# Bonus and decayed keys of two chunks formed on TensorE, and corner products in every chunk

## The chip, the cores and the metric

The kernel runs on one core of one Trainium2 chip. The metric is the device time of one execution in microseconds. A profile of one execution gives the busy times and waits of the engines: TensorE (PE, with its weight loads as PEld), VectorE (DVE), ScalarE (ACT), GpSimd (POOL) and SyncE (SP, which issues nearly all transfers here).

## What is computed

The reference is an attention layer with a decaying state, followed by a feed-forward network (FFN) with a maximum over three products. There are 4 batches, 8 heads, 768 tokens and 48 features a head; the FFN goes from 384 to 768 and back.

```python
for t in range(S):
    kt, vt, rt = (k[:, :, t], v[:, :, t], r[:, :, t])
    cur = np.einsum('bhd,bhe->bhde', u[None] * kt, vt)
    y[:, :, t] = np.einsum('bhd,bhde->bhe', rt, state + cur)
    state = w[None, :, :, None] * state + np.einsum('bhd,bhe->bhde', kt, vt)
...
h = np.maximum(np.maximum(x @ w1, x @ w2), x @ w3)
return (h @ w_out).astype(np.float32)
```

## The kernel before, in words

The 768 tokens are cut into 12 chunks of 64 tokens. Within a chunk the recurrence is written as products of matrices. Keys and receptances are scaled by powers of w (`kT`, `rT`, "by feature": features on partitions, tokens along the row). Their product is the **scores**, of which the strict triangle is kept; on the diagonal stands the **bonus**, the sum over features of r u k for one token. The **values** are the masked scores times v, plus the receptances times the state of the chunk before. The **keys** step multiplies keys that are decayed to the chunk's end (by token: tokens on partitions) with v and adds the product to the decayed state.

A chunk's work is done in two halves q, each of two head pairs and four batches, so eight units; one unit's two heads lie on partitions 0 to 63 and 64 to 127.

- Chunks 0 and 1 (`c < WHOLE`) are computed in float32 by `whole` (L514): for each unit two matmuls, on the upper left and the lower right corner of the array.
- From chunk 2 on, each operand is split into a high and a low half-precision part, and `split` forms three products of them. For `c < CORNERS`, 2 to 5, it does this on the two corners too (L507). For chunks 6 to 11 it does one matmul on the whole array (L504), with the stationary operand laid out as two blocks on a diagonal (`kb`, `ktb`, `vb`, `sb`); SyncE spreads it there from `kd`, `ktd`, `vd`, `sd` by two transfers each (`spread`, L403).
- The bonus of every chunk is formed by token: `product` (L468, L469: r times u, times k), `total` (L473: the sum over features) and `diagonal` (L482, or on ScalarE in chunks 1 and 2 L480), which writes a tile `am` with the sum on the diagonal. `mask` (L529) then copies the strict triangle of the scores into it.
- The decayed keys are formed by token: `decay` (L488) multiplies k with a table `tkt`. This table is made at the start from powers of w: `tkf`, four transposes on TensorE (`turn`, L381), and a scaled copy back on ScalarE (`turned_back`, L387).
- For each half `load_feat` fetches k and r by feature, and `load_tok` k, r and v by token.
- `into_state` takes the keys into the state (for chunk 0 a copy on ScalarE, L555). The tile `state` is cleared once by GpSimd (L422), as the last of the clearings that begin the program.
- `x_high` and `x_low` (L579, L583) leave the values as two half-precision parts in x; `x_last` (L590) moves the last rows by six small transfers.
- The FFN of a chunk is 162 matmuls up and 54 down, each 128x256 (L606), 216 together. The eight weight blocks arrive as float64 words and are turned into high and low half-precision parts by `tops`, `convert`, `round_up` and `leave` (L332, L336, L339, L342); three buffers hold the raw words.
- `stir` (L602) issues matmuls on zeros that fill TensorE early in the program.

The order of the work on every engine is laid down by a planner written in the kernel, `Plan`. Each step has a due time, an engine and a cost; the step that can begin first is taken, and among those that can begin together the one with the least due time. A table `SHIFT` moves the due times of a kind of step in five stages of the program. Attention of chunk c + 1 is planned among the FFN matmuls of chunk c. In the program each engine then takes its own steps in that order, and waits for what the next step in it needs.

Of the kernel before, what the change touches and what calls it, by code (L numbers as in the profile page):

```python
# [7 lines left out]
F32 = mybir.dt.float32  # L8
# [10 lines left out]
P = 128  # L19
# [9 lines left out]
CORNERS = 6  # L29
# [42 lines left out]
class Plan:  # L72
# [7 lines left out]
        "sp feat": (-1.49, 2.17, 0.19, -3.89, 0),  # L80
        "sp tok": (-1.09, 1.99, -1.51, 4.86, 0),
        "pe blank": (-0.88, 0, 0, 0, 0),
        "pe turned": (-0.6, 0, 0, 0, 0),
        "act tkt": (-3.41, 0, 0, 0, 0),
        "dve kT": (-1119.88, -1756.78, 0, 0, 0),
        "dve rT": (-1334.71, -15, 3.25, 0, 0),
        "dve am": (-1125.06, 1.34, 2.16, 2.05, -2.59),
        "dve a": (-2132.64, 1.4, 16.62, -0.32, 3.81),
        "pe sc": (0.03, -10.26, 30.66, -0.53, 1.03),
        "pe va": (0.91, 1.78, -0.08, 0.01, 0.84),  # L90
        "act xh": (-8.58, -4.39, 1.75, 1.33, -5.9),
        "dve xl": (16.85, -38.36, -0.44, -3.2, 5.06),
        "sp x3": (0.32, -1.77, -0.27, 5.34, 0),
        "act xsq": (0, 6.53, -0.6, 3.25, 26.15),
        "pe stir": (0, 0.37, 2.53, -0.41, -0.95),
        "sp word": (-0.57, -0.37, 0, 0, 0),
        "act ztop": (-7.39, -7.43, 0, 0, 0),
        "dve word": (-7.71, -14.92, 0, 0, 0),
        "act his": (58.47, -2.11, 0, 0, 0),
        "dve lo": (-35.68, -11.65, 0, 0, 0),  # L100
        "dve kdec": (-2131.57, 30.7, -5.18, 0, 0),
        "pe ke": (16.12, -0.08, -1.91, 0.38, 0),
        "act state": (0, -9.9, 0, 0, 0),
        "act sq": (0, -89.13, 2.23, 16.37, 24.01),
        "dve sd": (0, 2.02, 0, 0, 0),
        "act am": (0, 4.85, 3.9, 0, 0),
        "dve state": (0.52, 9.7, 0.2, -1, 0),
        "act sdh": (-0.93, -1.27, -0.92, 3.4, 0),
        "dve sdl": (-2.26, -11.65, -8.71, 1.59, 0),
        "pe up": (0, -2.28, 0, 0.17, 16.73),  # L110
        "act m": (0.86, 0.59, 4.26, -3.44, 1.05),
        "dve m": (5.69, -20.85, 12.62, -4.02, -0.89),
        "act hh": (0.73, -0.55, -2.83, -2.22, 1.5),
        "pool hl": (-0.73, -0.35, -5.98, -1.87, 1.73),
        "dve hl": (0, 1.96, -1.92, -1.11, -5.26),
        "pe dn": (0, -9.28, -5.13, 0.33, 0.9),
        "act io": (0, 1.12, -0.87, 1.27, 0.35),
        "sp io": (0, 0.08, -3.87, -0.2, 0.45),
        "act kdh": (0, 0.19, 6.03, 1.49, 1.44),
        "dve kdl": (0, -5.27, -1.57, 0.94, 3.23),  # L120
        "act rh": (0, 2.85, 1.75, 8.52, -0.79),
        "dve rl": (0, 3.84, -1.29, 6.17, -0.44),
        "act ah": (0, -1.76, 6.26, 15.54, 3.78),
        "dve al": (0, 0.87, 2.5, -0.18, 2.31),
        "act ktdh": (0, -6.24, 14.69, -1.38, 0),
        "dve ktdl": (0, 10.62, -0.11, -0.11, 0),
        "act vdh": (0, 5.83, 4.84, 9.54, 0.19),
        "dve vdl": (0, 0.77, 6.47, 1.1, -3.32),
        "pool kT": (0, 0, -0.51, -11.37, 0),
        "pool rT": (0, 0, -5.5, -2.61, 0.38),  # L130
        "pool am": (0, 0, -6.41, -29.97, -0.42),
        "pool kdec": (0, 0, 3.41, 2.45, 0),
        "sp sb": (0, 0, 0, -3.01, 0),
        "sp kb": (0, 0, 0, -8.27, 4.47),
        "sp ktb": (0, 0, 0, 0.67, 0),
        "sp vb": (0, 0, 0, 0.11, -1.09),
        "act wsq": (0, 0, 0, 7.12, 0),
        "sp again": (0, 0, 0, 0, 3.09),
        "dve ends": (0, 0, 0, 0, 2.23),
        "dve good": (0, 0, 0, 0, -0.78),  # L140
        "pe count": (0, 0, 0, 0, -2.69),
        "dve flag": (0, 0, 0, 0, -3.04),
# [99 lines left out]
def kernel(ctx, tc, feat, tok, wu, ut, ws, wo, cst, out):  # L242
# [34 lines left out]

    wu_sb = const.tile([P, 2, NP], F32, name="wu_sb")
# [105 lines left out]
    def turned_back():  # L384
        for hh in range(2):
            hs = slice(hh * C, (hh + 1) * C)
            nc.scalar.mul(out=tkt[hs], in_=turned[0][hs, :, hh * C:hh * C + D], mul=SC_KT)  # L387
# [138 lines left out]

    def mask(c, q):
        t = raws[c, q]
        nc.vector.copy_predicated(out=t["a"], mask=strict.unsqueeze(1).broadcast_to([P, U, C]), data=t.pop("sc"))  # L529
# [254 lines left out]
    plan = Plan(dict(feat=2, tok=3, raw64=3, psa=2, psv=2, psm=4, rh=2, rl=2, am=2, a=2, ah=1, al=1, x=2, m=3, io=3, hh=1, hl=1))  # L784
# [99 lines left out]
    def whole_scores(c, q, due):  # L884
# [19 lines left out]
    def keyed(c, q, due, reads):  # L904
        do(due, "pe", 1.35 if c < WHOLE else 0.79 if c < CORNERS else 0.62, lambda: keys(c, q), reads=reads, takes=[("psv", ("ke", c, q))], counts=0.5 if c < WHOLE else 1.0)
# [13 lines left out]
    def valued(c, q, due, reads):  # L919
        reads = [*reads, *held(c, [("sdh", q), ("sdl", q)], ("sb", q))]  # L920
        do(due, "pe", 1.58 if c < CORNERS else 1.42, lambda: values(c, q), reads=[*reads, ("ah", c, q), ("al", c, q), ("rh", c, q), ("rl", c, q)], takes=[("psv", ("va", c, q))])
# [77 lines left out]
    for q in range(2):  # L999
        fetched(0, q, -3 + 0.1 * q)  # L1000
        do(-4, "pe", 1.0, blank, takes=[("psv", ("blank", q))])
    do(-0.55, "pe", 0.55, turn, takes=[("psa", "turned")])
    do(-0.54, "act", 0.7, turned_back, reads=["turned"], writes=["tkt"])
# [92 lines left out]
```

## Time and profile before

| What | Value |
|---|---|
| Median of 3 runs | 395.57 us (395.3 to 395.86) |
| Profiled execution, time | 395.38 us |
| Profiled execution, span | 393.6 us |
| PE busy | 373.2 us, 95% |
| DVE busy | 257.0 us, 65% |
| ACT busy | 240.0 us, 61% |
| POOL busy | 189.2 us, 48% |
| Mean granted TensorE clock | 0.983 |
| Moved by DMA | 70.56 MB |

The span goes from the first to the last instruction that the profile holds; the time of the execution has a little more around it. "Idle before" in a row is the time in which the engine waited in front of an instruction, and the name behind the arrow is what ended the wait. PE's ends are modelled, so starts of neighbouring rows are the better ruler.

### The profile page before, as it was taken

The page shows a single profiled execution, that of the slowest core. Times are in us where ns is not written, and L with a number is a line of the kernel's source. Part 1 is how long each engine was busy: PE and PEld are TensorE (multiplying, and loading weights), DVE is VectorE, ACT ScalarE, POOL GpSimd, SP SyncE. Part 2 cuts the span into 40 slices and gives each one's busy share as a digit, 9 for nine tenths or more (in the row PEclk, how much of TensorE's full clock was granted, in tenths as well). Part 3 has the DMA queues.
Part 4 walks back from the last instruction along what each step waited for, and adds up shares of the span by engine and source line. Part 5 has one row for each costly group of instructions (what it writes and reads, how often), then busy time and mean ns, then how long its engine had stood idle before and what let it go on. Part 6 is the DMA issues. An engine that isn't in the chain of part 4 may idle for free.

```text
span 393.6 us, 13760 instructions
## 1 busy us (share of the span) xinstructions
PE 373.2 (95%) x5780; PEld 332.4 (84%) x5780; DVE 257.0 (65%) x475; ACT 240.0 (61%) x622; POOL 189.2 (48%) x187
## 2 busy tenths in 40 slices
PE   4977799899999999999999999999999999999994
PEld 3866688788888888888999999999999999988883
DVE  7699889888857567676776757658559545232350
ACT  2376876696656556556666556646564954697621
POOL 9600112499897646656566656656748311011110
PEclk9996899999999999999999999999999999999998
DMA  8976380730623423484993996995997874822201
GB/s 293 418 257 244 127 339 15 254 130 10 199 81 113 153 70 99 146 207 124 272 276 108 254 295 166 255 278 160 279 294 194 231 183 90 271 78 84 75 2 48
DMA packets 25430, 70.56 MB, mean 179 GB/s; under 512 B 4368, under 2 KB 11536, under 8 KB 24336
## 3 DMA queue, kind: packets, MB, share of 16 engines
q1 hardware_dynamic: 25216, 69.51, 59.2%
q8 instruction: 47, 0.77, 0.8%
q14 instruction: 23, 0.19, 0.2%
q10 hardware_dynamic: 144, 0.10, 0.1%
HBM read 39.95 MB, written 4.72 MB: 113 GB/s over the span
## 4 chain that ended last, share of the span: by engine, by line
PE 80%; DVE 8%; ACT 5%; POOL 4%; issue 1%; ACTq 0%; POOLq 0%
PE psm L606 66%; PE psv L504 6%; PE psv L507 4%; DVE w L342 2%; PE psa L504 2%; ACT ztop L332 2%; PE psa L507 2%; DVE raw L336 2%; ACT w L339 1%; DVE feat L449 1%; ACT junk L432 1%; POOL ztop L323 1%; ACT am L480 1%; POOL ktd L398 0%; POOL vd L398 0%
## 5 line engine op out<-in xcount | busy, mean ns | idle before, releaser
L606 PEld LDWEIGHTS <-w 128*128 128x128 f16 x2592 | 250.3, 98 | 32.8 <-issue 2.7
L606 PE MATMUL psm<-x,w 128*128 128x256 f16 x1944 | 224.0, 274 | 2.2 <-ACT m L621 2.1
L634 POOL TENSOR_TENSOR hl<-m,hh 128x256 f16<-128x256 f32 x60 | 49.8, 830 | 149.1 <-ACT hh L628 145.4
L625 DVE SCALAR_TENSOR_TENSOR m<-psm,m 128x256 f32<-128x256 f32 x144 | 60.4, 421 | 58.5 <-PE psm L606 48.6
L628 ACT CAST hh<-m 128x256 f16<-128x256 f32 x72 | 29.0, 402 | 57.3 <-DVE m L625 56.6
L449 POOL TENSOR_TENSOR feat<-feat,wrt 128x512 f32<-128x512 f32 x36 | 51.2, 1434 | 12.2 <-DMA feat<-in_feat_dram 12.0
L606 PE MATMUL psm<-hh,w 128*128 128x256 f16 x432 | 56.3, 273 | 0.0
L432 ACT ACTIVATE junk<-tok 128x384 bf16<-128x384 f32 x72 | 37.3, 518 | 2.2 <-DMA tok<-in_tok_dram 1.4
L621 ACT ACTIVATE m<-psm 128x256 f32<-128x256 f32 x72 | 27.2, 379 | 11.8 <-PE psm L606 10.7
L606 PE MATMUL psm<-hl,w 128*128 128x256 f16 x216 | 33.4, 273 | 0.0
L468 POOL TENSOR_TENSOR am<-tok,u_sb 128x384 f32<-128x384 f32 x18 | 18.4, 1020 | 20.1 <-DVE al L539 20.1
L583 DVE SCALAR_TENSOR_TENSOR x<-psv,x 112x512 f16<-112x512 f32 x24 | 16.4, 685 | 12.7 <-ACT x L579 12.6
L473 DVE TENSOR_REDUCE a<-am 128x8 f32<-128x384 f32 x24 | 13.2, 550 | 17.6 <-POOL am L469 17.5
L651 ACT ACTIVATE io<-psm 128x256 f32<-128x256 f32 x36 | 13.4, 382 | 16.8 <-PE psm L606 16.5
L482 POOL TENSOR_TENSOR am<-cs,a 128x512 f32<-128x512 f32 x18 | 19.7, 1092 | 7.6 <-DVE a L473 7.3
L529 DVE COPY_PREDICATED am<-cs,psa 128x512 f32<-128x512 int32 x24 | 17.5, 731 | 8.8 <-PE psa L504 7.2
L579 ACT ACTIVATE x<-psv 112x512 f16<-112x512 f32 x24 | 14.2, 590 | 12.4 <-PE psv L504 6.4
L417 DVE TENSOR_TENSOR kd<-feat,kd 128x512 f16<-128x512 f32 x20 | 18.9, 946 | 3.5 <-ACT kd L412 3.4
L469 POOL TENSOR_TENSOR am<-am,tok 128x384 f32<-128x384 f32 x18 | 18.9, 1047 | 1.4
L488 POOL TENSOR_TENSOR tok<-tok,tkt 128x384 f32<-128x384 f32 x16 | 18.6, 1162 | 0.5 <-ACT junk L432 0.5
L417 DVE TENSOR_TENSOR ktd<-tok,ktd 128x384 f16<-128x384 f32 x18 | 15.3, 850 | 4.9 <-DMA sb<-sd 2.3
L412 ACT ACTIVATE kd<-feat 128x512 f16<-128x512 f32 x20 | 12.5, 627 | 8.8 <-POOL feat L449 8.8
(110 smaller groups left out, 604.9 us busy)
## 6 DMA issues: line engine op xcount, KB each, us to landing
tok<-in_tok_dram SPq DMA_DIRECT2D x30, 576.0 KB, 5.9
feat<-in_feat_dram SPq DMA_DIRECT2D x24, 512.0 KB, 4.3
raw<-in_ws_dram SPq DMA_DIRECT2D x6, 1152.0 KB, 7.8
out_dram<-io SPq DMA_DIRECT2D x36, 128.0 KB, 4.6
kb<-kd SPq DMA_DIRECT2D x12, 256.0 KB, 6.4
sb<-sd SPq DMA_DIRECT2D x12, 256.0 KB, 6.7
vb<-vd SPq DMA_DIRECT2D x12, 256.0 KB, 7.5
kb<-kd SPq DMA_DIRECT2D x12, 248.0 KB, 6.6
```

What stands on the lines that cost most here:

```text
L417: nc.vector.tensor_tensor(out=dense.dense[:, 1, :, 0:w], in0=src, in1=dense.dense[:, 0, :, 0:w], op=ALU.subtract)
L432: nc.scalar.activation(out=junk[:, 0:U * D].rearrange("p (u d) -> p u d", u=U), in_=src, func=AF.Square, scale=scale, accum_out=stat[:, ki ...
L449: helper(c).tensor_tensor(out=t[n], in0=t[n], in1=tb, op=ALU.mult)
L469: helper(c).tensor_tensor(out=w, in0=w, in1=units(t["k"]), op=ALU.mult)
L482: helper(c).tensor_tensor(out=t["a"], in0=eye.unsqueeze(1).broadcast_to([P, U, C]), in1=t.pop("sum").unsqueeze(2).broadcast_to([P, U, C]), ...
L504: nc.tensor.matmul(out=ps[:, i, :], lhsT=block[k].on[a][i], rhs=prods[k](b, i), **flags)
L507: nc.tensor.matmul(out=ps[h][0:n, i, :], lhsT=dense[k].dense[h, a, i, 0:n], rhs=prods[k](b, i)[h], **flags)
L606: nc.tensor.matmul(out=ps, lhsT=a, rhs=b, start=first and n == 0, stop=last and n == len(prods) - 1)
L621: nc.scalar.mul(out=m, in_=ps, mul=by)
L625: nc.vector.scalar_tensor_tensor(out=m, in0=ps, scalar=by, in1=m, op0=ALU.mult, op1=ALU.max)
L628: nc.scalar.copy(out=h[0][:, f, :], in_=m)
L634: lows_by(c, f).tensor_tensor(out=h[1][:, f, :], in0=m, in1=h[0][:, f, :], op=ALU.subtract)
```

## The change

For chunks 0 and 1 neither k nor r is loaded by token; only v is (`load_v`). The bonus is formed by TensorE from the operands by feature: `r_u` multiplies the scaled receptances with u w (on ScalarE), `bonus` multiplies the scaled keys with that (32 float32 matmuls for each half), and `on_diagonal` keeps the diagonal of the result (on VectorE). The decayed keys by token are formed by `flipped`, a float32 product of the scaled keys with a diagonal matrix `dg`, and copied and scaled by ScalarE (`flipped_back`). `product`, `total`, `diagonal` and `decay` remain for chunks 2 to 11, and `tkf`, `turn` and `turned_back` become steps of the plan with later due times.

`CORNERS` goes from 6 to 12, so that `split` uses corners in every chunk from 2 on and no operand is spread any more. The clearing of the blocks kb, ktb, vb and sb by GpSimd stays. Costs of several steps in the plan and the whole table `SHIFT` are new.

```diff
-CORNERS = 6
+CORNERS = 12
...
     SHIFT = {
-        "sp feat": (-1.49, 2.17, 0.19, -3.89, 0),
...
+        "sp feat": (1.97, 1.58, -2.27, 4.37, 0),
...
+    def load_v(c, q):
+        t = raw.tile([P, 2, B, D], F32, name="v1", bufs=4)
+        nc.sync.dma_start(out=t, in_=tok[c, q][:, 2])
+        raws.setdefault((c, q), {}).update(v=t)
...
-    tkf = hp.tile([P, NP, 2, C], F32, name="hl")
-    for hh in range(2):
-        nc.vector.tensor_tensor(out=tkf[:, :, hh, :], in0=pw[:, :, 0:C][:, :, ::-1], in1=pw[:, :, C // 2].unsqueeze(2).broadcast_to([P, NP, C]), op=ALU.mult)
+    uw = const.tile([P, NP], F32, name="uw")
+    nc.vector.tensor_tensor(out=uw, in0=uf_sb, in1=w_sb, op=ALU.mult)
+    dg = const.tile([P, NP, D], F32, name="dg")
+    nc.vector.tensor_tensor(out=dg, in0=eye[:, 0:D].unsqueeze(1).broadcast_to([P, NP, D]), in1=wc.unsqueeze(2).broadcast_to([P, NP, D]), op=ALU.mult)
+    tkf = const.tile([P, NP, 2, C], F32, name="tkf")
+
+    def both():
+        for hh in range(2):
+            nc.vector.tensor_tensor(out=tkf[:, :, hh, :], in0=wkt, in1=wck.unsqueeze(2).broadcast_to([P, NP, C]), op=ALU.mult)
...
+    def r_u(c, q):
+        t = raws[c, q]
+        t["ru"] = work.tile([P, U, C], F32, name="ru")
+        for g in range(2):
+            nc.scalar.mul(out=t["ru"][:, g * B:(g + 1) * B, :], in_=t["rT"][:, g], mul=uw[:, 2 * q + g:2 * q + g + 1])
+
+    def bonus(c, q):
+        t = raws[c, q]
+        t["bo"] = psa.tile([P, U, C], F32, name="psa")
+        whole(t["bo"], C, (units(t["kT"]), t.pop("ru")))
+
+    def on_diagonal(c, q):
+        t = raws[c, q]
+        t["a"] = work.tile([P, U, C], F32, name="am", bufs=2)
+        nc.vector.tensor_tensor(out=t["a"], in0=t.pop("bo"), in1=eye.unsqueeze(1).broadcast_to([P, U, C]), op=ALU.mult)
+
+    def flipped(c, q):
+        t = raws[c, q]
+        t["kp"] = psa.tile([P, U, D], F32, name="psa")
+        for i in range(U):
+            for h in HS:
+                nc.tensor.matmul(out=t["kp"][h, i, :], lhsT=units(t["kT"])[h, i, :], rhs=dg[h, 2 * q + i // B, :], start=True, stop=True)
+
+    def flipped_back(c, q):
+        t = raws[c, q]
+        t["kt"] = work.tile([P, U, D], F32, name="kt")
+        nc.scalar.mul(out=t["kt"], in_=t.pop("kp"), mul=SC_KT / SC_R)
...
-            whole(t["ke"], D, (units(t["k"]), units(t["v"])))
+            whole(t["ke"], D, (t.pop("kt"), units(t["v"])))
...
+        if c < WHOLE:
+            dma(due, lambda: load_v(c, q), 0.85, reads=behind, writes=["fetched"], takes=[("v1", ("tok", c, q))])
+            return
...
+        if c < WHOLE:
+            do(due - 0.30, "pe", 0.76, lambda: flipped(c, q), reads=[("feat", c, q), ("kT", c, q)], takes=[("psa", ("kp", c, q))], counts=0.5)
+            do(due - 0.30, "act", act(U * D), lambda: flipped_back(c, q), reads=[("kp", c, q)], takes=[("kt", ("kt", c, q))])
+            return [t, ("kt", c, q)]
...
-        before_mask(c, q, due)
+        do(due - 0.27, "act", 2 * act(U * C // 2), lambda: r_u(c, q), reads=[f, ("rT", c, q)], takes=[("ru", ("ru", c, q))])
+        do(due - 0.27, "pe", 0.96, lambda: bonus(c, q), reads=[f, ("kT", c, q), ("ru", c, q)], takes=[("psa", ("bo", c, q))], counts=0.5)
+        do(due - 0.26, "dve", 0.64, lambda: on_diagonal(c, q), reads=[("bo", c, q)], takes=[("am", ("am", c, q))])
...
-    do(-0.55, "pe", 0.55, turn, takes=[("psa", "turned")])
-    do(-0.54, "act", 0.7, turned_back, reads=["turned"], writes=["tkt"])
+    do(0.1, "dve", 0.7, both, writes=["tkf"])
+    do(0.12, "pe", 0.55, turn, reads=["tkf"], takes=[("psa", "turned")])
+    do(0.14, "act", 0.7, turned_back, reads=["turned"], writes=["tkt"])
```

More of the change, by code (lines that the diff above doesn't have):

```diff
@@ L79 @@
     SHIFT = {
-        "sp feat": (-1.49, 2.17, 0.19, -3.89, 0),
[L81 to L121, printed above, removed]
@@ L133 @@
[L133 to L142, printed above, removed]
+        "sp feat": (1.97, 1.58, -2.27, 4.37, 0),
+        "sp tok": (-3.45, -1.24, -1.61, 3.67, 0),
@@ new lines @@
+        "pe blank": (-2.18, 0, 0, 0, 0),
+        "dve tkf": (0, 1.52, 0, 0, 0),
+        "pe turned": (0, 0.11, 0, 0, 0),
+        "act tkt": (0, -0.35, 0, 0, 0),
+        "dve kT": (-0.86, -9.38, 0, 0, 0),
+        "dve rT": (7.54, 0.51, 8.81, 0, 0),
+        "act ru": (-0.05, -0.44, 0, 0, 0),
+        "pe bo": (-4.05, 1.51, 0, 0, 0),
+        "dve am": (0, 5.93, 5.68, -3.51, 0),
+        "pe sc": (-2.13, -0.6, -4.99, -0.28, -2.15),
+        "pe va": (0.51, -10.53, -1.39, 0.02, -0.01),
+        "act xh": (0, 1.96, -5.35, -1.01, -2.13),
@@ L143 @@
+        "act wsq": (0, 0, 0, -0.02, -0.56),
+        "sp again": (0, 0, 0, 0, 3.74),
+        "dve ends": (0, 0, 0, 0, 2.93),
+        "dve good": (0, 0, 0, 0, -11.99),
+        "pe count": (0, 0, 0, 0, 0.31),
+        "dve flag": (0, 0, 0, 0, -4.22),
     }
@@ L386, in turned_back @@
             hs = slice(hh * C, (hh + 1) * C)
-            nc.scalar.mul(out=tkt[hs], in_=turned[0][hs, :, hh * C:hh * C + D], mul=SC_KT)
+            nc.scalar.copy(out=tkt[hs], in_=turned[0][hs, :, hh * C:hh * C + D])
     class Block:
@@ L781, in general @@
                     put(m, leaving(ps, P, 1.0))
-    plan = Plan(dict(feat=2, tok=3, raw64=3, psa=2, psv=2, psm=4, rh=2, rl=2, am=2, a=2, ah=1, al=1, x=2, m=3, io=3, hh=1, hl=1))
+    plan = Plan(dict(feat=2, tok=3, raw64=3, v1=4, ru=1, kt=1, psa=2, psv=2, psm=4, rh=2, rl=2, am=2, a=2, ah=1, al=1, x=2, m=3, io=3, hh=1, hl=1))
     do = plan.do
@@ L892, in whole_values @@
         sbs = [("sd", q), ("rT", c, q), ("feat", c, q)] if c else []
-        do(due, "pe", 1.35 * (1 + (c > 0)), lambda: values(c, q), reads=[("am", c, q), ("tok", c, q), *sbs], takes=[("psv", ("va", c, q))], counts=0.5)
+        do(due, "pe", 0.92 * (1 + (c > 0)), lambda: values(c, q), reads=[("am", c, q), ("tok", c, q), *sbs], takes=[("psv", ("va", c, q))], counts=0.5)
         leave_x(c, q, due)
     def scored(c, q, due, reads):
-        do(due, "pe", *((1.75,) if c < WHOLE else (0.79,) if c < CORNERS else (0.72,)), lambda: scores(c, q), reads=reads, takes=[("psa", ("sc", c, q))], counts=0.5 if c < WHOLE else 1.0)
+        do(due, "pe", 0.96 if c < WHOLE else 0.8 if c < CORNERS else 0.72, lambda: scores(c, q), reads=reads, takes=[("psa", ("sc", c, q))], counts=0.5 if c < WHOLE else 1.0)
         do(due + 0.02, "dve", dve(U * C), lambda: mask(c, q), reads=[("sc", c, q)], writes=[("am", c, q)])
@@ L904, in keyed @@
     def keyed(c, q, due, reads):
-        do(due, "pe", 1.35 if c < WHOLE else 0.79 if c < CORNERS else 0.62, lambda: keys(c, q), reads=reads, takes=[("psv", ("ke", c, q))], counts=0.5 if c < WHOLE else 1.0)
+        do(due, "pe", 0.76 if c < WHOLE else 0.64 if c < CORNERS else 0.62, lambda: keys(c, q), reads=reads, takes=[("psv", ("ke", c, q))], counts=0.5 if c < WHOLE else 1.0)
         s = ("state", q)
@@ L920, in valued @@
         reads = [*reads, *held(c, [("sdh", q), ("sdl", q)], ("sb", q))]
-        do(due, "pe", 1.58 if c < CORNERS else 1.42, lambda: values(c, q), reads=[*reads, ("ah", c, q), ("al", c, q), ("rh", c, q), ("rl", c, q)], takes=[("psv", ("va", c, q))])
+        do(due, "pe", 1.43 if c < CORNERS else 1.42, lambda: values(c, q), reads=[*reads, ("ah", c, q), ("al", c, q), ("rh", c, q), ("rl", c, q)], takes=[("psv", ("va", c, q))])
         leave_x(c, q, due)
```

61 lines of the change are left out of this document (47 added, 14 removed).

## The prediction

> **What bounds the kernel now.** I read the page's totals, then the span cut into stages, then TensorE and ScalarE in order of time where the stages lose time, and last the chain in the steady part. The profiled execution took 395.38 us for a span of 393.6 us, so 1.8 us lie around the span, and its time is 0.2 us under the median of 395.57 us. The sum below is made against 395.38. A difference under 0.2%, 0.8 us, can't be told from none.
>
> First the page's total of TensorE and the stages (columns: stretch, length, busy time of PE, weight load, DVE, ACT and POOL with their instructions, granted clock, DMA share, GB/s).
>
> ```profile
> PE 373.2 (95%) x5780; PEld 332.4 (84%) x5780; DVE 257.0 (65%) x475; ACT 240.0 (61%) x622; POOL 189.2 (48%) x187
> 0.00:16.00 16.00, 10.54 (x113) 7.93 (x114) 11.63 (x29) 2.29 (x4) 15.45 (x21) 1.00 0.90 345
> 16.00:35.68 19.68, 14.47 (x277) 12.73 (x274) 17.13 (x25) 13.37 (x27) 0.00 (x0) 0.83 0.80 285
> 35.68:48.20 12.52, 10.40 (x153) 8.55 (x150) 10.41 (x13) 11.79 (x21) 0.01 (x1) 0.86 0.35 132
> 48.20:71.20 23.00, 22.37 (x288) 19.26 (x285) 21.02 (x38) 16.94 (x38) 4.78 (x5) 1.00 0.45 169
> 71.20:80.00 8.80, 7.68 (x238) 6.88 (x236) 6.56 (x15) 5.85 (x18) 5.35 (x5) 1.00 0.86 301
> 80.00:387.80 307.80, 307.73 (x4728) 277.00 (x4725) 190.28 (x361) 189.40 (x517) 163.64 (x157) 1.00 0.60 166
> ```
>
> From 80 us to 387.8 us TensorE is busy 307.73 of 307.80 us at full clock: no other engine and no transfer is waited for there, so this part gets longer by whatever is added to TensorE and can't be shortened by relief elsewhere. Before it lies the start: up to 35.68 us TensorE has no FFN work at all, and from there to 80 us it loses 44.3 - 10.4 - 22.4 - 7.7 = 3.9 us idle and some more at a clock of 0.86 up to 48 us. The change works on both parts: it takes work off the start, and turns chunks 6 to 11 in the steady part to corner products. So two numbers decide.
>
> **First number: corner products in chunks 6 to 11.** Chunks 2 to 5 already use them, so the trace holds both kinds. I cut two chunk periods of each, from one chunk's first scores to the next one's. The rows are of the FFN's line alone (columns: stretch, length, PE, weight load, clock, DMA share, GB/s); below them stand pieces of the chain, L507 for corners and L504 for whole-array products (start, us, what).
>
> ```profile
> 107.50:137.72 30.22, 24.52 (x217) 20.74 (x216) 1.00 0.35 120
> 137.72:168.00 30.28, 24.45 (x216) 20.73 (x216) 1.00 0.36 111
> 197.50:226.40 28.90, 24.39 (x216) 20.78 (x216) 1.00 0.80 209
> 226.40:255.39 28.99, 24.40 (x216) 20.79 (x216) 1.00 0.89 237
> ```
>
> ```profile
> 137.88 0.77 PE psa L507 x48
> 138.64 7.97 PE psm L606 x72
> 146.61 1.51 PE psv L507 x96
> 154.93 0.88 PE psa L507 x48
> ...
> 226.56 0.70 PE psa L504 x24
> 227.26 7.86 PE psm L606 x72
> 235.12 1.40 PE psv L504 x48
> ```
>
> Each of these four periods holds the same 216 to 217 FFN matmuls and one chunk's scores, keys and values, and TensorE is never idle. With corners a period is 30.22 and 30.28 us, with the whole array 28.90 and 28.99 us: 1.30 us more for a chunk. The pieces say where it goes: scores 0.77 or 0.88 us against 0.70, values 1.51 against 1.40, and the FFN stretch that runs up to a corner group is longer too, 7.97 us against 7.86 for the same 72 matmuls. So about 0.1 us is lost on entering corners and 0.1 us on leaving them; the products themselves are no quicker, because 96 corner matmuls run in pairs where 48 whole ones ran. Five chunks (6 to 10) cost 5 x 1.30 = 6.5 us. Chunk 11 forms no keys: two scores (0.07 to 0.18) and two values (0.11), with four entries of 0.11, some 0.9 us. Sum 7.4 us, all on the path. The bounds: where the new due times put two corner groups beside each other, one exit and one entry, 0.2 us, fall away. With two such joins in each of six chunks it is 7.4 - 2.4 = 5.0 us; with none where there was one before, 7.8 us.
>
> What the corners take away is the spreading transfers of kb, ktb, vb and sb in chunks 6 to 11 and their issue on SP. Nothing on TensorE waited for them between 80 us and the end (0.07 us idle in all), so I price that at nothing; if the cover went, the next late thing would be the out transfer of a chunk, which nothing waits for until the end. That sd and kd are now read by the products themselves and so come free later is the state of chunks 2 to 5 already, where TensorE doesn't idle either: nothing.
>
> **Second number: the start.** Which operations go and come, by form (busy us, mean ns of one), and two groups of transfers (count, KB each, median us from issue to landing):
>
> ```profile
> L468 DVE TENSOR_TENSOR am<-tok,u_sb 128x384 f32<-128x384 f32 x4 | 2.2, 550 | 0.0
> L469 DVE TENSOR_TENSOR am<-am,tok 128x384 f32<-128x384 f32 x4 | 2.2, 558 | 0.1
> L473 DVE TENSOR_REDUCE a<-am 128x8 f32<-128x384 f32 x4 | 2.2, 547 | 0.1
> L488 DVE TENSOR_TENSOR tok<-tok,tkt 128x384 f32<-128x384 f32 x4 | 2.2, 551 | 0.0
> L482 DVE TENSOR_TENSOR am<-cs,a 128x512 f32<-128x512 f32 x2 | 1.4, 684 | 0.0
> L529 DVE COPY_PREDICATED am<-cs,psa 128x512 f32<-128x512 int32 x4 | 2.9, 729 | 1.6 <-PE psa L514 1.1 <-ACT am L480 0.5
> L480 ACT ACTIVATE am<-cs,a 128x64 f32<-128x64 f32 x16 | 4.0, 338 | 3.4 <-DVE a L473 3.4
> L621 ACT ACTIVATE m<-psm 128x256 f32<-128x256 f32 x5 | 1.8, 376 | 0.0
> L412 ACT ACTIVATE sd<-state 128x384 f16<-128x384 f32 x2 | 1.0, 507 | 0.0
> L602 PE MATMUL psm<-still 128*128 128x256 f16 x90 | 12.7, 305 | 0.0
> raw<-in_ws_dram SPq DMA_DIRECT2D x3, 1152.0 KB, 11.3
> x<-x SPq DMA_DIRECT2D x72, 16.0 KB, 1.9
> ```
>
> VectorE loses, for each of four units (chunks 0 and 1, two halves), two products, a sum and a decay, 0.550 + 0.558 + 0.547 + 0.551 = 2.21 us, and for chunk 0 twice the spreading of the diagonal, 0.684: 8.8 + 1.4 = 10.2 us. It gains four products of the bonus with the diagonal, read from PSUM like the mask, 0.73 us: 2.9 us, and the small uw, wck and dg, under 0.7 us. ScalarE loses sixteen diagonal blocks, busy 4.0 us together; it gains eight r_u over 256 columns, 0.376 us: 3.0 us, and four flipped_back over 384 columns, 0.51 us: 2.0 us. SP issues the same number of transfers; k and r by token fall away in four of them, 4 x 384 KB, at 345 GB/s 4.6 us of transfer time, half of it ahead of the first weight blocks, which so land some 2 us earlier. I price that at nothing, for the reason in the next rows. On TensorE come bonus and flipped four times; the nearest rows are the same 32 matmuls of chunk 0.
>
> ```profile
> 17.87 1.10 PE L514 MATMUL psa<-feat 64*64 64x64 f32 x32
> 18.80 0.88 PE L514 MATMUL psv<-tok 64*48 64x48 f32 x32
> 28.14 1.56 PE L514 MATMUL psa<-feat 64*64 64x64 f32 x32 [2.08 <-issue]
> 32.00 1.52 PE L514 MATMUL psv<-tok 64*48 64x48 f32 x32 [2.30 <-issue]
> 35.68 4.10 PE L606 MATMUL psm<-x,w 128*128 128x256 f16 x36
> 16.02 0.54 ACT L555 COPY state<-psv 128x192 f32<-128x192 f32 x2 [7.71 <-POOL state L422]
> 17.12 1.48 ACT L332 CAST ztop<-raw 128x1152 f16<-128x1152 bf16 x1
> 24.40 0.68 DVE L583 SCALAR_TENSOR_TENSOR x<-psv,x 112x512 f16<-112x512 f32 x1
> 3.56 3.24 SPq L315 DMA_DIRECT2D raw<-in_ws_dram  x3
> 25.11 3.91 SPq L590 DMA_DIRECT2D x<-x  x6
> ```
>
> Bonus is 1.10 us and flipped 0.88 us, 4 x 1.98 = 7.9 us. For chunk 0 (4.0 us) they stand where 90 stirring matmuls (12.7 us) pass the time: nothing. For chunk 1 (4.0 us) they compete with the FFN. The powers' transposes (turn, turned_back) move behind the first fetches in the order; their product tkt is now read first by chunk 2's decay on VectorE, more than 35 us later, so the move costs nothing and takes work from ScalarE's first queue.
>
> What holds the start: ScalarE's copy of the first state waits 7.71 us for GpSimd's clearing of the state at 16.0 us, and the first weight block is behind it at 17.12 us, though blocks issued from 3.56 us and landing 11.3 us later by the median are there by about 15 us. The clearing isn't changed, so weights still begin at 17 us or later. The last x of chunk 0 is done at 24.40 + 0.68 us, its six x_last transfers are issued to 29.02 us and land 1.9 us later, so FFN could start at about 31 us. It starts at 35.68 us because in TensorE's order keys and scores of chunk 1 stand ahead of it (2.08 and 2.30 us idle at 28 and 32 us, half clock), which wait for VectorE: scaling, products, sum, decay.
>
> After the change I see x of chunk 0 about 3 us earlier. Its mask no longer stands behind a product chain of 2.2 us for each half, but its scores need one of two PSUM buffers, which flipped_back of the second half frees on ScalarE. That one needs the second half's keys, the state copy only the first half's, so it is likely to be queued behind the copy, not before 17 us; from there scores 1.1, mask 0.73, values as long as scores, x high and low some 0.7 each, with hand-overs 22 us, x_last to 26, landing 28 us. FFN then starts 7.7 us earlier than 35.68. Against that, scores and keys of chunk 1, which ran ahead of the FFN (at full clock 2 x 1.1 + 0.9 = 3.1 us), and its bonus and flipped, 4.0 us, now fall among the FFN's matmuls unless they get done before x lands. If all fall there and nothing else changes, the gain is 7.7 - 7.1 = 0.6 us. If none do, and the 3.9 us idle up to 80 us and the loss by the clock (0.14 x 12.52, 1.8 us) go as well, because VectorE has 3.5 us less to do in chunk 1 and the weights come sooner, it is 7.7 + 5.7 = 13.4 us. I take half of the 7.1 as hidden and the stalls as they are, since weights, buffers and ScalarE's order still set them: 7.7 - 3.5 = 4.2 us.
>
> **Sum.** 395.4 + 7.4 - 4.2 = 398.6 us, 0.8% slower.
>
> The granted clock is 0.83 from 16 to 35.68 us where TensorE has gaps. By the Trainium skill, TensorE: Matmul & The Clock Gate, Part 1, an idle window of 3.4 us brings the half clock; if TensorE waited from 20 to 28 us for x, the first such window of FFN would cost about 1.7 us of the gain as an estimate, which gives 400.3 us. The stage's 0.83 agrees that gaps are paid twice.
>
> **Rivals.** (a) The start gains more than the corners cost. Place: FFN of chunk 0 from 35.68 to 71.2 us. For it speaks that 35.5 us hold only 216 FFN matmuls, 23.6 us by 7.86 for 72, and a few products of chunks 1 and 2; against it that eight weight blocks must be turned to halves on ScalarE and VectorE (tops alone takes 1.48 us), from 17 us on, and that these two are busy most of that stretch already. It decides from a gain of 8.2 us; with 10.8 us, the middle between that and the bound, the time is 395.4 + 7.4 - 10.8 = 392.0 us. (b) The start gains nothing: the second half of chunk 0 and all behind it wait on ScalarE behind the state copy, weights slip by a second state copy (0.54 us) and the work that comes with it, and x is no earlier: 395.4 + 7.4 = 402.8 us. (c) The corner groups get joined by the new due times, 5.0 us, and the start gains 4.2: 396.2 us, or with 5 us gained no change: 395.4. (d) Corner products run at twice the rate in chunks 6 to 11. A chunk's attention is 28.95 - 23.6 = 5.4 us with the whole array; halved, it saves 2.7 us in each of five chunks and 2 in the last, 15 us: 395.4 - 15 - 4.2 = 376 us. In the Trainium skill, TensorEngine Tiling (Array Packing), section Theoretical Speedup gives up to twice the speed for a dimension of at most 64. The periods above contradict it for this pairing, 30.25 us against 28.95, so it gets 1 in 100. That the corners cost nothing because TensorE isn't the bound is excluded by the row from 80 us on.
>
> **How the numbers follow.** Forecast, 396.3 to 401 us: 0.48. (b), 401 us or more: 0.13. (c), within 0.8 us of before: 0.10. (a): 0.28. (d): 0.01. So slower 0.61, same 0.10, faster 0.29. The range reaches from 391.5 us, which leaves out nearly the better half of (a), 0.13, to 402.5 us, which leaves out 0.06 of (b): 0.2 with (d).
>
> **What would show it.** Right: the lines of split have no L504-like whole-array form left, chunk periods after 170 us take 30.2 us with 216 FFN matmuls, and TensorE idles nowhere behind 80 us. ScalarE's first state copy still ends near 16.5 us. The first FFN matmul is at 27 to 29 us, and the first matmul of chunk 1's FFN (71.2 us now, where the stages are cut) comes some 4 us earlier. Wrong: periods near 29 us (joined groups, or corners cheaper than in chunks 2 to 5); chunk 1's FFN beginning before 63 us (the start gains 8 us or more); or idle time on TensorE in the steady part, which none of my terms has.

## The result and the profile after

The changed kernel takes 402.1 us in the median of four executions (401.5, 401.6, 402.6 and 411.99), the kernel before 395.5 us beside it. It is slower by 6.6 us, where 3.2 us were forecast. The execution of 411.99 us is a slow one and is left out of the ratio, 1.0161 with a 95% interval of 1.014 to 1.0182; without it the median is 401.6 us, 6.1 us above the kernel before.

The profile of the changed kernel comes from the execution of 411.99 us, in which one small VectorE instruction stood 12 us; so only its steady part is read here, and the start is read from a kernel that differs in that instruction and the three like it alone (kernel A below). First that profile's DVE timeline (start us, us, engine, line, operation; in brackets the idle time before it and what ended it):

```profile
3.62 0.18 DVE L368 RECIPROCAL sc<-raw 128x4 f32<-128x4 f32 x1
3.83 12.10 DVE L369 TENSOR_SCALAR sc<-sc 128x4 f32<-128x4 f32 x1
15.96 0.42 DVE L371 TENSOR_TENSOR wrt<-raw,sc 128x256 f32<-128x256 f32 x1
```

The same instruction in the profile of before, same view:

```profile
3.82 0.79 DVE L363 TENSOR_SCALAR sc<-sc 128x4 f32<-128x4 f32 x1
4.64 0.42 DVE L365 TENSOR_TENSOR wrt<-raw,sc 128x256 f32<-128x256 f32 x1
```

Four numbers for each partition take 12.10 us in one execution and 0.79 us in another. The steady part of the changed kernel, as pieces of its chain (start, us, what):

```profile
165.32 0.77 PE psa L522 x48
166.09 6.00 PE psm L649 x54
...
195.52 0.77 PE psa L522 x48
...
225.71 0.77 PE psa L522 x48
```

A period is 30.20 and 30.19 us, as chunks 2 to 5 had it before, and no whole-array group is left.

### The profile page after: what moved, and what is told of

Same layout as the page of the kernel before. It is cut to its first block, busy times and chain, and to the rows that moved or that the text cites. A ratio compares the mean times of both kernels' runs of the same rounds, so it can differ in the third digit from the quotient of the medians.

```text
span 410.2 us, 16271 instructions
## 1 busy us (share of the span) xinstructions
PE 386.7 (94%) x7140; PEld 339.2 (83%) x7140; DVE 277.0 (68%) x464; ACT 242.6 (59%) x618; POOL 190.2 (46%) x187
## 4 chain that ended last, share of the span: by engine, by line
PE 88%; DVE 7%; issue 2%; ACT 0%; DMA 0%; DVEq 0%; ACTq 0%
PE psm L649 66%; PE psv L522 10%; PE psa L522 4%; DVE sc L369 3%; PE psm L645 2%; PE psv L529 2%; PE psa L529 2%; PE psa L563 1%; DVE feat L464 1%; DVE m L668 1%; DVE tok L503 0%; DMA wu_sb<-in_wu_dram 0%; ACT ztop L338 0%; DVE kd L432 0%; PE psa L396 0%
## 5 line engine op out<-in xcount | busy, mean ns | idle before, releaser
L464 POOL TENSOR_TENSOR feat<-feat,wrt 128x512 f32<-128x512 f32 x36 | 55.2, 1548 | 8.0 <-ACT ktd L427 8.0
L474 DVE TENSOR_TENSOR rl<-feat,rh 128x512 f16<-128x512 f32 x20 | 15.0, 749 | 33.0 <-ACT rh L469 33.0
L522 PE MATMUL psv<-ah,vd 64*48 64x64 f16 x640 | 30.0, 191 | 0.0
L522 PEld LDWEIGHTS <-vd 64*48 64x48 f16 x960 | 26.1, 101 | 4.7 <-issue 4.7
L522 PE MATMUL psv<-rh,sd 64*48 64x64 f16 x640 | 29.7, 190 | 0.0
L522 PE MATMUL psv<-al,vd 64*48 64x64 f16 x320 | 28.6, 190 | 1.0 <-issue 1.0
L522 PE MATMUL psv<-rl,sd 64*48 64x64 f16 x320 | 28.4, 190 | 0.0
L522 PEld LDWEIGHTS <-sd 64*48 64x48 f16 x960 | 26.1, 101 | 0.0
L694 ACT ACTIVATE io<-psm 128x256 f32<-128x256 f32 x36 | 13.0, 381 | 15.9 <-PE psm L649 15.7
L434 DVE SCALAR_TENSOR_TENSOR sd<-state,sd 128x384 f16<-128x384 f32 x20 | 22.1, 1105 | 0.4 <-ACT sd L427 0.3
L469 ACT CAST rh<-feat 128x512 f16<-128x512 f32 x20 | 12.3, 616 | 15.6 <-PE psv L522 15.6
```

Source lines behind the costliest of these rows:

```text
L434: nc.vector.scalar_tensor_tensor(out=dense.dense[:, 1, :, 0:w], in0=src, scalar=scale, in1=dense.dense[:, 0, :, 0:w], op0=ALU.mult, op1=AL ...
L464: helper(c).tensor_tensor(out=t[n], in0=t[n], in1=tb, op=ALU.mult)
L522: nc.tensor.matmul(out=ps[h][0:n, i, :], lhsT=dense[k].dense[h, a, i, 0:n], rhs=prods[k](b, i)[h], **flags)
```

## The experiments

**A chip that always holds.** The changed kernel unchanged (e0), its start alone (e1: `CORNERS = 6` in the changed kernel), and its corners alone (e2: `CORNERS = 12` in the kernel before) ran first on a chip on which the kernel before took 406.3 us instead of 395.5.

> The changed kernel as it is, for a second profile: the first one shows VectorE's tensor_scalar sc standing 12.1 us, until GpSimd's clearings end at 15.9 us. Theory A (the corners cost 7.4 us, the start gains a little over 1 us): a profile near 400 us in span, that instruction under 1 us, chunk periods 30.2 us, first FFN matmul near 35 us. Theory B (the late clearing holds VectorE in every execution): the instruction stands 12 us again.

> The changed kernel with CORNERS back at 6; TensorE's order is the same up to the first chunk that differs. Theory A (corners in chunks 6 to 11 cost 7.4 us as their periods of before say): 401.6 - 7.4 = 394.2 us, a little under before's 395.5. Theory B (the corners cost what the plan's costs give them, 0.22 us a chunk, 1.3 us in all, and the start loses some 5 us): 400.3 us.

> The kernel before with CORNERS at 12 and nothing else. Theory A: 395.5 + 7.4 = 402.9 us, with chunk periods of 30.2 us all through, and a profile like before's up to 168 us. Theory B: 395.5 + 1.3 = 396.8 us, 396 us if the transfers that go had held something.

Measured:

- e0: 411.56 us (one run).
- e1: 408.77 us in the median (407.29 without three executions above 412 us), ratio 1.0031 (1.0003 to 1.0059).
- e2: 416.4 us, ratio 1.0269 (1.0233 to 1.0304); one more execution took 1346.74 us and is left out.

The small operation stood 12.10, 12.09 and 12.11 us in the three profiles, as theory B of e0 had it. e2 is 10.1 us above the kernel before, so the plan's own 1.3 us for the corners is out. e1 shows no gain, but it also waits 3.9 us for the transfers of kb and ktb, which have no due times of their own there, and with everything behind the hold the start can't be sized. The next kernels remove the hold.

**Without the hold.** The operations on four numbers become products with constant tiles, in both kernels (before's form is called B here and f1 in the expectations, the changed kernel's form A and f2; the cut shows the first of the operations):

```diff
-    nc.vector.tensor_scalar(out=sc, in0=sc, scalar1=SC_R, scalar2=None, op0=ALU.mult)
+    by = const.tile([P, 3, NP], F32, name="by")
+    for n, x in enumerate((SC_R, SC_V, SC_KT / SC_R)):
+        nc.vector.memset(by[:, n], x)
+    nc.vector.tensor_tensor(out=sc, in0=sc, in1=by[:, 0], op=ALU.mult)
...
```

and then each with the other's value of `CORNERS` (f3 and f4; for A with 6, the four `sp` rows of before's due times are put back):

> The kernel before, with VectorE's three small tensor_scalar and copy instructions at the start (4 numbers for each partition) written as tensor_tensor with constant tiles. Theory L (such an instruction can't start while GpSimd clears, and is let in after one clearing in some executions and only after the last, at 15.9 us, in others): it takes under 0.3 us everywhere, and the kernel runs at 393.5 to 395.5 us on any chip, also on one where the kernel before takes 406 us; the gain there is 10 us or more. Rival S (that chip is slower as a whole): 404 to 406 us there.

> The changed kernel with the same edit. Theory L with a small start gain (1.3 us, as 401.6 us says): 400 to 401.5 us. Theory L2 (the changed start does gain 4 us and more, and the wait at the clearings has eaten it in the executions of 401.6 us too): 396 to 398.6 us.

> The kernel before with that edit and CORNERS at 12: the corners alone. Price of 7.4 us from the chunk periods: 7.4 us over f1; the profile of e2 shows 1.1 us of new idle time on TensorE behind 150 us, so 8.5 us with due times that were made for spread operands. Rival (the plan's own 1.3 us): 1.3 us over f1.

> The changed kernel with that edit and CORNERS back at 6, with the due times of the spreading transfers as before had them: the changed start alone. Price of 7.4 us: 7.4 us under f2, so 393 to 394 us with a small start gain and 389 to 391 us under L2. It may lose 1 to 3 us of this to waits in the chunks from 6 on, whose due times weren't made for spread operands.

| Kernel | Median us | Ratio to before |
|---|---|---|
| B | 395.87 | 0.9994 (0.9969 to 1.0019) |
| A | 400.58 | 1.0113 (1.0056 to 1.0169) |
| B, corners everywhere | 405.08 | 1.0218 (1.0165 to 1.0272) |
| A, whole array in 6 to 11 | 398.4 | 1.0043 (1.001 to 1.0076) |

The operation now takes 0.16 us, and none of the 14 timed executions of A and B shows the 10 us of the hold; B is as fast as the kernel before, 0.4 us above the 393.5 to 395.5 us that were expected, so B and A stand for the two kernels. A's 400.58 us is the number of theory L; L2, a larger gain that the hold had eaten, is out. Neither ran on the chip that always holds, so rival S, that this chip is slower as a whole, was not tried; that e2 is there 11.3 us above f3, about the length of the hold, speaks against it. Corners everywhere add 9.2 us to B, of which its waits of TensorE behind 150 us explain some:

```profile
PE psm L609 <- issue: 1.4, 3, 0.8
```

(engine and line, what it waited for, us in total, times, longest). From the first scores of chunk 6 to the start of the last group of FFN matmuls B takes 218.85 us, B with corners 227.50; less 1.36 us of those waits that is 7.3 us for the corners. The last kernel of the table missed its 393 to 394 us; it waits for transfers that the corners had made needless:

```profile
PE psa L526 <- DMA kb<-kd: 3.0, 2, 2.8
PE psv L526 <- DMA ktb<-ktd: 1.6, 2, 1.3
```

Without these 4.6 us it would be at 393.8 us, 6.8 us under A, which agrees with the price of the corners.

**What of the corners costs.** In B, corners in chunks 6 to 11 for the values alone (k1), and for scores and keys alone (k2). Theory W: each change between corner and whole-array matmuls costs; rival M: each corner matmul does.

```diff
 CORNERS = 6
+UNTIL = {'kb': 6, 'ktb': 6, 'vb': 12, 'sb': 12}
...
-                if c >= CORNERS:
+                if c >= until:
...
```

> f1 (the kernel before, without VectorE's wait) with corners in chunks 6 to 11 for the values only; scores and keys stay on the whole array. Twelve groups of 96 corner matmuls. Theory W (the price is paid on each change between corner and whole-array matmuls, 0.11 us in and 0.11 us out): 12 x 0.22 = 2.6 us over f1 behind 150 us, net of idle time. Rival M (it is paid on each corner matmul: 7.4 us over 1152 + 1056 of them): 3.9 us.

> f1 with corners in chunks 6 to 11 for scores and keys only; values stay on the whole array. Twelve groups of scores and ten of keys, 48 corner matmuls each, some of them beside one another. Theory W: 12 x 0.23 + 10 x 0.2 = 4.8 us, less 0.2 for each pair that stands together, so 3.5 to 4.8 us net of idle time, more than k1. Rival M: 3.5 us, less than k1.

Measured: 400.75 us, ratio 1.011 (1.0061 to 1.0158), and 403.86 us, ratio 1.0186 (1.0145 to 1.0227). Both profiles are 2.1 us behind B at chunk 6 already (first scores at 170.4 us against 168.3), which isn't the corners'; so the same stretch is compared: 221.44 us, 2.6 more than B, and 223.29, 4.4 more. W asked for 2.6 and 3.5 to 4.8, M for 3.9 and 3.5, so M is out. One period of each, from the chains: B with corners everywhere, values only, scores and keys only (in the last two L508 is the whole array, L511 corners).

```profile
198.83 0.77 PE psa L510 x48
...
229.02 0.77 PE psa L510 x48
```

```profile
200.14 0.70 PE psa L508 x24
200.84 7.86 PE psm L610 x72
208.70 1.51 PE psv L511 x96
210.21 5.02 PE psm L610 x45
...
229.56 0.70 PE psa L508 x24
```

```profile
200.38 0.77 PE psa L511 x48
201.15 7.97 PE psm L610 x72
209.11 1.40 PE psv L508 x48
210.51 4.91 PE psm L610 x45
...
230.14 0.77 PE psa L511 x48
```

The periods are 30.19, 29.42 and 29.76 us; over the whole array's 28.95 that is 1.24, 0.47 and 0.81, and the parts add up to within 0.04. The same 72 FFN matmuls read 7.86 us ahead of whole-array scores and 7.97 ahead of corners: the 0.1 us lies at the change. In the Trainium skill, TensorEngine Tiling (Array Packing), section Key Properties, changing the tiling mode drains TensorE. No run here shows the drain itself, but the price falls on the changes as that would have it: about 0.11 us going in and 0.1 coming out.

**What holds the start.** A with `state` cleared as the first of GpSimd's clearings instead of the last ("A early", g1); A with two stirring matmuls a call instead of three (g5); and B with the early clearing, the control ("B early", g2).

```diff
+    state = const.tile([P, NP, B, D], F32, name="state")
+    nc.gpsimd.memset(state, 0.0)
     ztop = [const.tile([P, WN], I32, name=f"ztop{h}") for h in range(2)]
...
-    state = const.tile([P, NP, B, D], F32, name="state")
-    nc.gpsimd.memset(state, 0.0)
```

> f2 (the changed kernel, no wait of VectorE at the clearings) with one more edit: GpSimd clears the state first and the other tiles after it, instead of last at 15.9 us. Theory P (in the changed start everything behind the first state copy waits for that clearing: the copy on ScalarE 3.4 us, behind it VectorE's scaling of the state 3.6 us, behind that on_diagonal of the second half, and so x): state copy near 12.5 us, tops of the first weight block near 13 to 14 us instead of 17.05, last x_low near 21 us instead of 23.9, and 1.5 to 3 us less in all, 397.5 to 399 us against 400.6. Rival Q (the FFN's start at 36.3 us is held by TensorE's own queue: products of chunk 1 ahead of it and a stall of 2.5 us in the middle of a bonus group): state copy and weights earlier, FFN within 0.7 us of 36.3 and the time within 0.7 us of f2.

> f2 with two matmuls in each stir instead of three: 60 instructions fewer on TensorE ahead of chunk 1. In f2, f4 and both profiles of the changed kernel, TensorE stands 1.4 to 2.5 us after the 24th of 32 matmuls of the bonus of chunk 1, where nothing has to be waited for. Theory I (the next block of its instructions had not arrived, while weights filled the transfers): the stall moves by 60 instructions, out of this group into the FFN's first matmuls or the group behind, and gets shorter there; FFN begins near 33.8 us. Rival D (it waits for data): the stall stays between the same two matmuls. Time 398 to 400.6 us by I, 400.6 us by D.

> The kernel before with the four-number operations of VectorE as products of two tiles, and in addition GpSimd clears the tile state as the first of its clearings instead of the last. Theory P (the late clearing costs only where something ahead of the FFN is queued behind the state copy on ScalarE or the scaling of the state on VectorE; in the changed kernel that is on_diagonal of the second half, before the change nothing of that kind: the bonus stands on VectorE ahead of it and x_low is set by the chain of products, scores and masks): under 1 us of gain, 394.9 to 395.9 us, first FFN matmul at 35 us or later. Rival Q2 (the late clearing holds the start of both kernels alike, by ScalarE's weights behind the copy): some 4 us of gain, about 391.5 us, first FFN matmul near 31 us.

Measured: A early 399.48 us (394.14 to 400.93), ratio 1.008 (1.0043 to 1.0116); A with fewer stirs 398.89 (one execution of 748.47 among its ten), ratio 1.0065 (1.0035 to 1.0094); B early 394.23 us, ratio 0.9952 (0.9932 to 0.9972), faster than the kernel before. The control decides against theory P in one point: I had expected under 1 us there, since I believed that nothing of before's was queued behind the clearing. It gains 1.6 us on B; rival Q2 has the place right and its 4 us too large. A early's median misses theory P's 397.5 to 399 us and is 1.1 us under A, a difference that the intervals of the two ratios don't separate from none; its start moved as P had it. VectorE's timelines of B and of A, and then ScalarE's of A, show what waits:

```profile
16.60 0.36 DVE L917 TENSOR_SCALAR state<-state 128x384 f32<-128x384 f32 x1 [1.95 <-ACT state L558]
...
18.56 1.36 DVE L336 SCALAR_TENSOR_TENSOR raw<-raw,ztop 128x1152 int32<-128x1152 int32 x1 [1.13 <-ACT ztop L332]
19.84 0.72 DVE L532 COPY_PREDICATED am<-cs,psa 128x512 f32<-128x512 int32 x1
...
24.33 0.69 DVE L586 SCALAR_TENSOR_TENSOR x<-psv,x 112x512 f16<-112x512 f32 x1
```

```profile
16.60 0.36 DVE L967 TENSOR_SCALAR state<-state 128x384 f32<-128x384 f32 x1 [3.58 <-ACT state L601]
16.87 0.68 DVE L559 TENSOR_TENSOR am<-psa,cs 128x512 f32<-128x512 f32 x1
18.55 1.36 DVE L342 SCALAR_TENSOR_TENSOR raw<-raw,ztop 128x1152 int32<-128x1152 int32 x1 [1.00 <-ACT ztop L338]
19.83 0.72 DVE L575 COPY_PREDICATED am<-cs,psa 128x512 f32<-128x512 int32 x1
...
23.90 0.68 DVE L629 SCALAR_TENSOR_TENSOR x<-psv,x 112x512 f16<-112x512 f32 x1
```

```profile
15.95 0.54 ACT L601 COPY state<-psv 128x192 f32<-128x192 f32 x2 [3.44 <-POOL state L440]
...
17.05 1.47 ACT L338 CAST ztop<-raw 128x1152 f16<-128x1152 bf16 x1
```

In both kernels VectorE stands in its queue at the scaling of the state until 16.60 us, behind ScalarE's copy (15.95 us in both), behind GpSimd. Then it waits again, for ScalarE's tops of the first weight block, which are queued behind that copy and end at 18.5 us; the first step of rounding these weights (`raw<-raw,ztop`) stands ahead of the second half's mask. So the mask follows at 19.84 and 19.83 us, and the last x at 24.33 and 23.90. The time saved ahead of 16.60 us is only a longer wait, 3.58 us instead of 1.95. With the early clearing A goes on without these waits (same view; below it B early's last x):

```profile
14.45 0.69 DVE L559 TENSOR_TENSOR am<-psa,cs 128x512 f32<-128x512 f32 x1 [0.99 <-PE psa L532]
...
16.32 0.73 DVE L575 COPY_PREDICATED am<-cs,psa 128x512 f32<-128x512 int32 x1
...
20.96 0.68 DVE L629 SCALAR_TENSOR_TENSOR x<-psv,x 112x512 f16<-112x512 f32 x1
```

```profile
21.87 0.69 DVE L586 SCALAR_TENSOR_TENSOR x<-psv,x 112x512 f16<-112x512 f32 x1
```

So with the early clearing A's last x is 0.91 us ahead of B's, with the late one 0.43. On TensorE the FFN of chunk 0 starts at 36.30 us in A, at 31.24 in A early, at 33.24 in B early. In A, its last products ahead of the FFN also stop in the middle of a group, and with fewer stirs they don't (TensorE's timelines of A and of A with fewer stirs):

```profile
32.51 0.88 PE L532 MATMUL psa<-ru,feat 64*64 64x64 f32 x24
35.92 0.45 PE L532 MATMUL psa<-ru,feat 64*64 64x64 f32 x8 [2.54 <-issue]
36.30 4.10 PE L652 MATMUL psm<-x,w 128*128 128x256 f16 x36
```

```profile
32.06 1.11 PE L532 MATMUL psa<-ru,feat 64*64 64x64 f32 x32
33.11 2.58 PE L652 MATMUL psm<-x,w 128*128 128x256 f16 x22
36.63 1.59 PE L652 MATMUL psm<-x,w 128*128 128x256 f16 x13 [0.94 <-issue]
```

Nothing on another engine is waited for, and the stop has moved by exactly as many matmuls as were left out: 90 stirs became 60, and it comes 8 + 22 = 30 matmuls later, each a weight load and a matmul. A early stops at the same place as A, for only 0.34 us. So the stop belongs to a place in TensorE's instruction stream, not to an operand. Of the 5.1 us by which A early's FFN begins sooner than A's, 2.9 are earlier work and 2.2 the shorter stop. The Trainium skill, Runtime: NRT & Kernel Launch, section Instruction fetch mechanics, has instructions fetched in blocks of 256 with a cost that is mostly hidden. A stop at a fixed place in the stream agrees, but no run shows that the place is the edge of such a block; and if it is a fetch, 0.94 to 2.54 us of idle TensorE aren't hidden. That the fetch is late because transfers fill the queues then (DMA share 0.67 from 16 to 35.68 us) was not tried.

**The start without the corners' price.** A early with `CORNERS = 6`, and due times of A in the first two stages of the table, of B in the other three ("mixed", g3); the same with the late clearing (g3b); mixed with the first three stages of A (h2); and A's own due times with whole array and early clearing (h3).

> The changed kernel's start, whole-array products in chunks 6 to 11 (CORNERS = 6), the due times of the changed kernel in the first two stages of the table and those of the kernel before in the other three, the four-number operations as products of two tiles, state cleared first. Theory P with the corner price of 7.4 us: the steady part is that of the kernel before, without waits on the spreading transfers, and the start gains 4 to 7 us: 388 to 391.5 us, under both kernels. Rival S (the start's gain is tied to the steady part's due times: what is gained ahead of 80 us comes back as idle time of TensorE behind it): 393 us or more, with over 2 us idle on TensorE behind 80 us.

> The same mixed kernel with the state cleared last, as in the kernel before. Theory P: the start gains only the 3 us that the changed kernel showed, so about 4 us above the mixed kernel with the early clearing, 391.5 to 394 us, first FFN matmul near 36 us. Rival Q2 and rival S: no difference of more than 1.5 us between the two mixed kernels.

> The mixed kernel with the early clearing again, the due times of the changed kernel now in the first three stages of the table (all of chunks 0 to 1) and those of the kernel before in the last two. The mixed kernel lost 6.3 us idle on TensorE between 85 and 150 us, where scores of chunk 3 waited for the low part of r. Theory T (the loss came from the place where the two tables meet, and the start by itself is worth its gain): under 2 us idle behind 85 us, 389 to 392 us, under the kernel before with the early clearing (394.23). Rival S (what the start gains comes back as idle time wherever the tables meet): over 3 us idle behind 85 us, 394 us or more.

> The changed kernel with whole-array products in chunks 6 to 11 under its own due times (398.4 before), with the state cleared first in addition. If the early clearing is worth what it was worth in the kernel before (1.6 us) and the 4.6 us idle behind 150 us, on the spreading transfers, stay: 396.8 us. If the idle time goes with the new order: 392 us. Rival S: 398 us or more.

| Kernel | Median us | Ratio to before |
|---|---|---|
| mixed | 399.41 | 1.0062 (1.0033 to 1.0092) |
| mixed, late clearing | 402.98 | 1.0161 (1.0132 to 1.019) |
| mixed, three stages of A | 390.47 | 0.9871 (0.9831 to 0.9912) |
| A early, whole array | 399.75 | 1.0109 (1.0059 to 1.0158) |

My first mixture missed its 388 to 391.5 us: it was put together so that chunk 3's operands come late. From 85 to 150 us (columns as in the prediction's stages), it and then the third kernel:

```profile
85.00:150.00 65.00, 58.69 (x1189) 50.70 (x1187) 39.80 (x69) 35.94 (x94) 39.28 (x37) 0.92 0.24 76
```

```profile
85.00:150.00 65.00, 64.08 (x1286) 56.26 (x1285) 48.29 (x83) 40.29 (x110) 49.21 (x45) 1.00 0.34 102
```

6.3 us idle in the one, 0.9 in the other, and 3.6 us of the waits of the first name rl and rh, which the scores read:

```profile
PE psa L529 <- DVE rl L481: 2.0, 2, 1.7
PE psa L529 <- ACT rh L476: 1.6, 1, 1.6
```

So it was the place where the two tables meet, as theory T had it, and the third kernel beats both: 1.3% under the kernel before. It still idles 2.3 us behind 150 us, so theory T's "under 2 us idle behind 85 us" isn't met, though its time is. The late clearing costs the mixture 3.6 us, about what theory P had: on one chip, with the first FFN matmul at 36.50 us instead of 33.26, the clearest of the three pairs. The last kernel is where rival S's number came true, but by the spreading transfers (kb 3.2 us, ktb 3.0 us of waits), which come too late under A's due times.

## Why the prediction was right in its direction and wrong in its size

**Corners, +7.4 us: right.** The periods are 30.2 us as forecast, the price is the change of mode, and the same order with corners costs 7.3 us net. Rival (c) is out by the periods of the changed kernel, which have every entry and exit; (d) is out by more than 25 us.

**No idle TensorE in the steady part: nearly.** A is busy 306.89 of 307.80 us behind 80 us, 0.9 us idle; B with corners under before's own due times idles 1.4 us there.

**The start, -4.2 us: this step failed.** The changed kernel gained 7.4 - 6.6 = 0.8 us (1.3 us by the median of 401.6); A against B, 7.4 - 4.7 = 2.7 us, with an interval of 2.2 us to either side. The stages of A, cut as in the prediction:

```profile
16.00:35.68 19.68, 14.85 (x350) 12.96 (x346) 15.28 (x21) 14.80 (x23) 0.00 (x0) 1.00 0.67 240
35.68:48.20 12.52, 12.28 (x255) 11.08 (x256) 10.94 (x14) 10.08 (x18) 1.38 (x1) 1.00 0.41 129
48.20:71.20 23.00, 22.77 (x289) 19.88 (x288) 21.71 (x35) 17.23 (x38) 7.13 (x6) 1.00 0.60 213
71.20:80.00 8.80, 8.39 (x200) 7.38 (x198) 7.71 (x15) 7.28 (x23) 4.78 (x5) 1.00 0.33 107
80.00:387.80 307.80, 306.89 (x5760) 270.67 (x5759) 203.34 (x357) 187.04 (x507) 160.39 (x155) 1.00 0.26 89
```

The sub-steps came out the other way round from how I had them. I put the gain in an earlier x ("about 3 us earlier", FFN at 28 us) and left the stalls as they were. In A the last x is 0.43 us earlier than in B and the FFN starts at 36.30 us, later than the 35.68 before. What A gains comes behind that: from 35.68 to 80 us TensorE idles 44.32 - 43.44 = 0.9 us instead of 3.9, at a clock of 1.00 instead of 0.86, with part of chunk 1's products done ahead of the FFN. By 71.20 us the kernel before had come to its 226th FFN matmul (the last ten are chunk 1's, whose first stands at 65.79 us, not at 71.2 as I had it); A comes to it at 68.2 us. This row is where chunk 1's FFN begins in A:

```profile
67.19 2.14 PE L652 MATMUL psm<-x,w 128*128 128x256 f16 x18
```

That is 3.0 us sooner, where I had forecast some 4 us. That it comes so near in A is luck: the one gain I had counted, the earlier x, is not what brings it, and what brings it are the stalls and the clock, which I had left as they were.

My row for what holds the start was the right one, ScalarE's copy at 16.02 us behind the clearing. I followed it down ScalarE's queue, to a `flipped_back` that would free a PSUM buffer for the second half's scores at 17 us. TensorE's timeline of A has those scores before the copy, and the second half's flipped product behind them:

```profile
14.22 1.43 PE L532 MATMUL psa<-feat 64*64 64x64 f32 x32
...
17.61 1.14 PE L566 MATMUL psa<-dg,feat 64*64 64x48 f32 x32 [1.06 <-DVE am L559]
```

What I left out is VectorE's queue. There the scaling of the state waits for the same copy, with on_diagonal behind it, and the rounding of the first weight block waits for ScalarE's tops behind that copy, with the mask and x_low behind it. The bonus and the scores that on_diagonal and the mask read were there by 15.65 us.

With the late clearing taken away in both kernels and whole-array products in both, the change's start is worth 0.8% in ratios to before (0.9952 to 0.9871, on two chips), 3.2 us, give or take 1.8, and 3.8 us by the medians (394.23, 390.47): close to the 4.2 that I had forecast for a kernel in which the late clearing stayed. Even there x is not the 3 us earlier that I had counted (0.91 us in A early against B early). That form carries due times of both kernels and 2.3 us of idle time behind 150 us, so another form may give more or less.

**Rival (b)**, start gains nothing, 402.8 us, is the nearest case, and for its reason: work behind the state copy. I gave it 0.13 because I thought the chain of products, and not this clearing, set x before the change. Rival (a) needed 8.2 us of gain; no version's median gained that. Only the fastest execution of A early did, 7.4 + 1.9 = 9.3 us, and by its profile chunk 1's FFN begins there at 61.72 us, before the 63 us that the prediction named for (a).

**Open.** A early took 394.14 us at a mean granted clock of 0.998 and up to 400.93 at 0.986, so its median gains only 1.1 us on A while its profile, of the fastest execution, gains 5.9 us of span. What lowers the clock in the others isn't in that profile. And whether the 1.9 us between the changed kernel (0.8 gained) and A (2.7) are its operations on four numbers is not shown: the two were not timed side by side, and the intervals of their ratios overlap. At like clocks they are nearly the same: 402.6 us at 0.986 against 402.48 at 0.987, and 401.5 and 401.6 at 0.993 against 401.0 at 0.994. So, in these few executions, most of that difference goes with the clock; what sets the clock is open.

## What to carry to other kernels

When a chain of work is shortened, find the last thing that every engine's queue on that chain waits for, in program order, not only the engine whose row shows the longest wait; if that event isn't moved, the saving turns into a longer wait in front of it (1.95 us became 3.58). Try the one-line move of that event in the unchanged kernel too: here clearing one tile first gained 0.5% without the change, where the rewritten operations alone gained nothing. A price per change of mode is read from the neighbours of the short groups, and a change that mixes a gain with a known loss should be split before it is timed.

## What was not expected of the hardware

A VectorE `tensor_scalar` of four numbers per partition, begun at 3.83 us, ended only when GpSimd's last clearing did, at 15.9 us; GpSimd's timeline of that execution shows memsets back to back:

```profile
2.73 1.84 POOL L413 MEMSET kd<- 128x1024 f32 x2
...
15.17 0.74 POOL L437 MEMSET state<- 128x768 f32 x1
```

On one chip every profile shows it (before took 406.3 us there, the changed kernel 411.56), elsewhere only that of the execution of 411.99 us; the same work as a product of two tiles took 0.16 us and stood in no profile, though it didn't run on that chip. In the Trainium skill, SBUF — State Buffer, section Who interferes with whom, `tensor_scalar` can use a port pair that VectorE shares with GpSimd, whoever issues first keeps it for its instruction, and a product of two tiles doesn't contend with a GpSimd that only writes. The runs agree on which form stands; that the port pair is the cause no run shows. That the loser waits through more than a dozen memsets in a row, 12.1 us, and not through one of 0.9 us (1.84 us for two), is what they add; it is not so each time, since the same instruction took 0.79 us beside the same memsets in the profile of before.
